# DeltaNet and a gated MLP on one core: chunk 0's inverses joined by matrix products, its scores a slot later, weight conversions redistributed

## The chip, the cores and the metric

The kernel runs on one core of a Trainium2 chip. The metric is the device time of one execution in microseconds. TensorE (PE; its weight loads are shown apart as PEld), VectorE (DVE), ScalarE (ACT), GpSimd (POOL) and the DMA queues that SyncE (SP), ACT and POOL issue run side by side. Each engine works off its own queue in order and waits for the others by semaphores.

## The reference

Two stages follow each other. The first is a delta-rule recurrence over 768 steps for 4 batches of 8 heads, with head size 48; the second is a two-layer MLP over the 3072 resulting rows, 384 to 2048 to 384, with a sigmoid-gated unit:

```python
k_n = k / (np.linalg.norm(k, axis=-1, keepdims=True) + 1e-06)
for t in range(S):
    kt, vt, bt = (k_n[:, :, t], v[:, :, t], beta[:, :, t, None])
    y[:, :, t] = np.einsum('bhd,bhde->bhe', q[:, :, t], state)
    v_old = np.einsum('bhde,bhd->bhe', state, kt)
    state = state + bt[:, :, :, None] * np.einsum('bhd,bhe->bhde', kt, vt - v_old)
...
h = x @ w_in
g = h * (1.0 / (1.0 + np.exp(-1.702 * h)))
return (g @ w_out).astype(np.float32)
```

The inputs `w_in` and `w_out` arrive as 64-bit floats and have to be turned into 32-bit ones on the chip.

## The kernel before

**Tiling.** The 768 steps are cut into 6 chunks of 128 steps. A *unit* is one chunk of one batch with all 8 heads; there are 24, ordered by chunk and then batch, so units 0 to 3 are chunk 0. Within a chunk the recurrence is a triangular system. It is cut into four blocks of 32 steps: a block's right-hand side V is multiplied by the inverse of the block's own 32x32 triangle (`solve`, tile psU, copied to U), and what U contributes to the later blocks is computed by `below` (psR) and subtracted from V by `rest`.

**Inverses.** `prepare` transposes the normalised keys (psT to kT), forms G, the products of keys with keys (psG), and sends G through DRAM so that the 32x32 blocks on its diagonal land in NT, one block to a partition: 32 partitions a batch (8 heads times 4 blocks). `invert` works on NT with VectorE. It scales NT by beta (L402), builds the inverses of both 16x16 halves of every block by a recursion of 15 steps (L424 to L431), and then joins the halves: the lower left quarter of NT is multiplied by one half's inverse (loop at L439) and the result by the other's (loop at L448), each in four pieces of one product and one reduction. The result times beta (L460, tile YS) is stored to DRAM (Yd) and loaded as XB, laid out so that `solve` can use it as weights. For chunk 0 all four batches are inverted at once before the loop, for later chunks two batches at a time, in pieces between other work.

**Scores.** `Step.scores` transposes a unit's queries (psT to QS), forms the masked products of keys and queries (psQ, copied to M, masked by a GpSimd select at L532). In later chunks it takes the state's contribution off V too (L527). `outputs` turns M and U into the unit's result (psY), which goes to xT; the rows that don't fit the copy's layout go through small DMAs on SP (L617).

**Slots.** The main loop runs over slots n = -1 to 24. Slot n has six groups; three units are in it at different points: A = unit n-1, B_ = unit n, D_ = unit n+1. D_'s scores are made in groups 0 to 2, its first block is solved in group 3; B_'s second block in group 1, third in group 5, and the last two blocks, the outputs and the state fall to it as A in the next slot. After each group come pieces of the inversion for the next chunk, `left // (GR - group)` weight conversions, and MoE matmuls worth the slot's share of time; with no MoE work queued, up to slot 2, six filler matmuls on a constant (`warm`). In slots -1 to 1 the order of the engines' instructions is pinned as written (`Engine`, L108); later, a scheduler may move them.

**Weights.** w_in is cut into 12 raw parts of 512 columns by 128 rows, w_out into 16 of 128 rows. A raw part is fetched by `ahead` into a staging place, most of these inside the still unused w_out tile, and `convert` turns it into 32-bit floats: `begin` issues the first step (L181) and an ACT relu (L186), the rest is four VectorE instructions (L190 to L193). A place can be fetched into again once its part is converted. `W0` parts are converted while the keys are prepared, `W1` just before the loop, `WB[n + 1]` in slot n. `hidden` (ph, L633) and `written` (po, L648) are the two MoE products; the first pair of units has its hidden products in slots 2 and 3 and its output products from slot 3 on.

**Order before the loop.** After the keys, units 0, 1 and 2 are scored, two more converted parts follow, the raw loads of the next six w_in parts are queued on SP, then chunk 0 is inverted, keys 4 to 6 are normalised (`normalize_first`), and the loop begins.

Of the kernel before, what the change touches and what calls it, by code (L numbers as in the profile page):

```python
# [8 lines left out]
F32 = mybir.dt.float32  # L9
# [9 lines left out]
def kernel(  # L19
# [35 lines left out]
    FQ = 4  # L55
    GB = 4

    W0, W1, WB = 3, 1, (1, 3, 5, 7, 8)
    NA = W0

    NW, NA0, NY, NB0 = 80, 3, 48, 6
# [331 lines left out]
    def invert(c, b0=0, nb=B):  # L393
# [37 lines left out]
            yield 0.0  # L431


        X1 = N[:, 0:HS, HS:]
        act.activation(X1, halves(Y)[1].rearrange("p l i -> p i l"), ACT.Copy)
        A = N[:, 0:HS, 0:HS]
        N10, Y0 = N[:, HS:, 0:HS], halves(Y)[0]
        Q = 4
        for j in range(0, HS, Q):  # L439
            n = HS - j  # L440
            dots(
                A[:, j : j + Q, :],
                N10[:, :, j:].rearrange("p (o l) k -> p o l k", o=1).broadcast_to([np, Q, HS, n]),
                Y0[:, j : j + Q, j:].rearrange("p j (o k) -> p j o k", o=1).broadcast_to([np, Q, HS, n]),
                Q, HS, n, False,
            )
            yield 0.0
        for i in range(0, HS, Q):  # L448
            n = i + Q
            dots(  # L450
                Y[:, 0:HS, HS + i : HS + i + Q],
                A[:, :, 0:n].rearrange("p j (o l) -> p j o l", o=1).broadcast_to([np, HS, Q, n]),
                X1[:, i : i + Q, 0:n].rearrange("p (o i) l -> p o i l", o=1).broadcast_to([np, HS, Q, n]),
                HS, Q, n, True,
            )
            yield 0.0
# [25 lines left out]
    class Step:  # L482
# [15 lines left out]

        def rows(self, h):
            return slice(h % 2 * 64, h % 2 * 64 + D)  # L500

        def scores(self):

# [190 lines left out]

    steps, xTs, inverting, gT0 = {}, {}, iter(()), []

    class NoStep:
        scored = iter(())

        def __bool__(self):  # L700
            return False

    def new_step(n):
        if n >= len(units):
            return NoStep()
# [22 lines left out]
    def slot(n, share):  # L728
# [81 lines left out]
    for b in range(B + 1):  # L810
# [14 lines left out]
    for U in US:  # L825
        nc.gpsimd.memset(U[:, H * D :], 0.0)
    for i in range(B, len(KN)):
        nc.gpsimd.memset(KN[i][:, :, D:DP], 0.0)
    for i in range(B, len(KN)):
        load(i, ((KN, k),), sync)  # L830
# [39 lines left out]
```

## Time and profile before

| | us |
|---|---|
| median of 13 runs | 834.96 |
| lowest and highest | 831.92, 839.08 |
| the profiled execution | 836.03 |
| its span, first to last instruction | 834.3 |

| engine | busy us | share of the span |
|---|---|---|
| PE | 782.4 | 94% |
| PEld | 574.8 | 69% |
| DVE | 493.2 | 59% |
| ACT | 214.1 | 26% |
| POOL | 119.1 | 14% |

A share over the whole span mixes stages. The first 66.5 us prepare keys and inverses, the loop's first slots solve chunk 0, from 104.5 us on TensorE has MoE products to do as well. The lines are to be read by stage: which engine is full there, and what the others wait for. "Granted clock" is the share of its full clock at which TensorE was allowed to run.

### The profile page before, as it was taken

To read this page: it belongs to the slowest core of one execution; us is meant where nothing else is said; L and a number is where in the kernel's file an instruction comes from. 1 tells how busy PE (TensorE), PEld (TensorE's weight loads), DVE (VectorE), ACT (ScalarE), POOL (GpSimd) and SP (SyncE) were. 2 spreads that over 40 slices of the span, in tenths; PEclk is the share of its full clock that TensorE was granted. 3 is DMA by queue.
4 is the path that set the end of the run, shared out by engine and by line. 5 is a ranking of instruction groups with operands and counts; after the bars stand their busy time and mean duration, and the time that the engine had idled before them with its cause. 6 is when DMAs were issued, how large, how long until landed. Compare 5 with 4: busy or idle time off the path is not lost.

```text
span 834.3 us, 18791 instructions
## 1 busy us (share of the span) xinstructions
PE 782.4 (94%) x8100; PEld 574.8 (69%) x8100; DVE 493.2 (59%) x1095; ACT 214.1 (26%) x441; POOL 119.1 (14%) x138
## 2 busy tenths in 40 slices
PE   8338899879999999999999999999999999999998
PEld 6327788546867867867867767767767768677684
DVE  6898889688776395394494493593692871110000
ACT  2303543232322321312312212222223212111020
POOL 2103120232022112102202202202200000000000
PEclk9659698988999999999999999999999999999999
DMA  9996731722214204213213223123123020000000
GB/s 148 197 169 137 194 86 48 181 65 68 56 35 107 61 11 101 61 30 82 62 45 73 55 52 78 43 58 88 27 56 78 1 60 2 11 15 2 24 1 19
DMA packets 147315, 55.97 MB, mean 67 GB/s; under 512 B 114336, under 2 KB 143232, under 8 KB 147232
## 3 DMA queue, kind: packets, MB, share of 16 engines
q1 hardware_dynamic: 139488, 41.96, 24.6%
q0 software_dynamic: 2752, 10.62, 4.5%
q10 hardware_dynamic: 4992, 2.20, 1.0%
q8 instruction: 63, 1.03, 0.5%
q14 instruction: 20, 0.16, 0.1%
HBM read 33.13 MB, written 20.45 MB: 64 GB/s over the span
## 4 chain that ended last, share of the span: by engine, by line
PE 68%; DVE 15%; DMA 7%; issue 7%; POOL 3%; ACT 0%; ACTq 0%; DVEq 0%; SPq 0%; POOLq 0%
PE ph L633 26%; PE po L648 24%; PE psU L552 4%; PE psY L568 4%; PE psQ L519 2%; PE psG L366 2%; DMA KN<-in_k_dram 2%; DVE P L426 2%; DVE YB L430 2%; DVE P L104 2%; DMA w_out<-in_moe_w_out_dram 2%; PE psR L541 2%; POOL rn L312 1%; DMA w_out<-in_moe_w_in_dram 1%; PE psS L590 1%
## 5 line engine op out<-in xcount | busy, mean ns | idle before, releaser
L633 PE MATMUL ph<-xT,w_in 128*128 128x256 f32 (+1 forms) x1248 | 278.0, 376 | 2.6 <-DMA xT<-last 2.4
L648 PE MATMUL po<-w_out,gT 128*128 128x384 f32 x768 | 267.9, 495 | 4.7 <-DVE w_out L193 4.6
L633 PEld LDWEIGHTS ph<-xT,w_in 128*128 128x128 f32 x1248 | 222.8, 196 | 41.3 <-issue 9.4
L648 PEld LDWEIGHTS po<-w_out,gT 128*128 128x128 f32 x768 | 140.4, 190 | 95.1 <-DVE w_out L193 6.9
L638 ACT ACTIVATE gT<-ph 128x512 f32<-128x512 f32 (+1 forms) x104 | 58.7, 565 | 190.1 <-PE ph L633 190.0
L548 DVE TENSOR_TENSOR V<-V,psR 32x384 f32<-32x384 f32 x87 | 48.3, 555 | 89.9 <-PE psR L541 88.2
L552 PEld LDWEIGHTS psU<-V,XB 32*32 32x32 f32 x1408 | 52.0, 106 | 35.0 <-issue 17.2
L559 ACT COPY US<-psU 32x384 f32<-32x384 f32 x88 | 41.4, 470 | 130.5 <-PE psR L541 112.7
L552 PE MATMUL psU<-V,XB 32*32 32x48 f32 x1408 | 63.4, 205 | 5.6 <-DVE V L527 4.2
L532 POOL TENSOR_SCALAR_AFFINE_SELECT M<-M 128x1024 f32<-128x1024 f32 x24 | 27.3, 1137 | 265.9 <-DVE M L529 192.9
L541 PE MATMUL psR<-US,G 32*32 32x48 f32 x2080 | 60.9, 204 | 0.0
L655 DVE COPY o<-po 128x384 f32<-128x384 f32 x24 | 13.1, 544 | 66.9 <-PE po L648 66.8
L541 PEld LDWEIGHTS psR<-US,G 32*32 32x32 f32 x2080 | 50.2, 105 | 1.4 <-issue 1.2
L426 DVE TENSOR_TENSOR P<-NT,YB 64x2 f32<-64x2 f32 (+4 forms) x135 | 46.8, 347 | 4.0
L430 DVE TENSOR_REDUCE YB<-P 64x2 f32<-64x2 f32 (+4 forms) x135 | 43.3, 321 | 4.3
L519 PE MATMUL psQ<-QS,kT 48*128 48x176 f32 (+1 forms) x384 | 42.9, 350 | 2.1 <-ACT QS L352 2.1
L527 DVE TENSOR_TENSOR V<-V,psQ 128x96 f32<-128x96 f32 x80 | 17.4, 250 | 40.4 <-PE psQ L519 39.7
L519 PEld LDWEIGHTS psQ<-QS,kT 48*128 48x128 f32 x384 | 30.8, 206 | 14.3 <-issue 4.8
L529 ACT COPY M<-psQ 128x256 f32<-128x256 f32 x68 | 23.9, 374 | 65.1 <-DVE V L527 60.3
L89 POOL DMA_DIRECT2D KN<-in_k_dram x14 | 13.4, 957 | 185.5 <-PE psS L590 174.4
L609 DVE COPY last<-psY 128x128 f32<-128x128 f32 x20 | 5.8, 288 | 52.6 <-PE psY L568 52.4
L153 PE MATMUL ps_warm<-ident 128*128 128x256 bf16 x152 | 21.1, 302 | 15.8 <-DVE ps_warm L104 13.5
(118 smaller groups left out, 795.9 us busy)
## 6 DMA issues: line engine op xcount, KB each, us to landing
Nd<-G SPq DMA_DIRECT2D x20, 512.0 KB, 3.2
w_out<-in_moe_w_out_dram POOLq DMA_DIRECT2D x14, 384.0 KB, 3.8
QP<-in_q_dram SPq DMA_DIRECT2D x24, 192.0 KB, 3.1
V<-in_v_dram SPq DMA_DIRECT2D x24, 192.0 KB, 2.9
out_dram<-o SPq DMA_DIRECT2D x24, 192.0 KB, 2.8
w_out<-in_moe_w_in_dram SPq DMA_DIRECT2D x6, 576.0 KB, 11.9
NT<-Nd SPq DMA_DIRECT2D x24, 128.0 KB, 2.6
Yd<-YS SPq DMA_DIRECT2D x24, 128.0 KB, 2.2
```

The source lines that it names most:

```text
L426: tt(P, diag(Nf, i * BS, [[0, i], [1, i]]), diag(Yf, 0, [[BS, i], [1, i]]), op=ALU.mult,)
L430: red(diag(Yf, i, [[BS, i]]), P, axis=AX.X, op=ALU.add, negate=True)
L519: pe.matmul(ps[hh][:, i, 0:n], lhsT=self.kT[r, g + i, :], rhs=self.QS[r, g + i, 0:n], start=True, stop=True,)
L532: nc.gpsimd.affine_select(out=self.M, in_=self.M, compare_op=ALU.is_gt, fill=0.0, base=0, pattern=[[0, H], [1, 128]], channel_multiplier=-1,)
L541: pe.matmul(psR[u, h, :], lhsT=self.G[r, h, u], rhs=self.U[r, h, :], start=True, stop=True,)
L548: vec.tensor_tensor(self.V[u], self.V[u], psR[u], op=ALU.subtract)
L552: pe.matmul(psU[r, h, :], lhsT=inverse[self.n][r, h, :], rhs=self.V[r, h, :], start=True, stop=True,)
L559: act.copy(self.U[r], psU[r])
L568: pe.matmul(self.psY[h % 2][p : p + DP, s, :], lhsT=lhsT(h), rhs=rhs(h), start=start and s == 0, stop=True, skip_group_check=True,)
L633: pe.matmul(ph[:, u], lhsT=w_in[:, j, f * 128 : (f + 1) * 128], rhs=xT[:, j, t], start=(j == 0), stop=(j == KC - 1),)
L638: act.activation(gT[f0 // FQ][:, f0 % FQ : f0 % FQ + 2, t], ph, ACT.Gelu_apprx_sigmoid)
L648: pe.matmul(po, lhsT=gT[f // FQ][:, f % FQ, i * C : (i + 1) * C], rhs=w_out[:, f, :], start=(f == 0), stop=(f == FC - 1),)
```

## The change

- In `invert`, chunk 0 skips the join of the halves: no copy of the transposed half to NT, none of the eight product and reduction pairs. YS then holds the two 16x16 inverses of each block, scaled by beta, and goes to DRAM and back to XB as before.
- A new generator, `Step.merged`, joins the blocks of a unit of chunk 0 from XB: a transposition of XB in 32x32 blocks on VectorE (XT), 32 small products of G with the second half (psA), a copy (A), 32 products with the transposed first half (psA again), and four activations with scale -1 that write the missing quarter into XB.
- In slot n, when unit n+1 is of chunk 0, its join is begun in group 0 and finished in group 1.
- Units of chunk 0 are scored in slot n as B_ rather than in slot n-1 as D_, so nothing is scored ahead of the loop. In slot 3 unit 3 and unit 4, the first of chunk 1, are scored in the same groups.
- Ahead of the inversion stand one load of three raw parts, keys 4 to 6 and the values of two units; another three raw parts, the queries and the other values come after the inverses' own transfers. Before, six raw parts, all queries, all values and keys 4 to 6 were ahead.
- Conversions: W1 = 2 instead of 1, WB = (3, 4, 4, 5, 7) instead of (1, 3, 5, 7, 8). With W0 = 3 both sum to 28.

```diff
-    W0, W1, WB = 3, 1, (1, 3, 5, 7, 8)
+    W0, W1, WB = 3, 2, (3, 4, 4, 5, 7)
...
+        Q = 4
+        quarters = range(0, HS, Q) if c > 0 else ()
         X1 = N[:, 0:HS, HS:]
-        act.activation(X1, halves(Y)[1].rearrange("p l i -> p i l"), ACT.Copy)
+        if c > 0:
+            act.activation(X1, halves(Y)[1].rearrange("p l i -> p i l"), ACT.Copy)
...
-        for j in range(0, HS, Q):
+        for j in quarters:
...
-        for i in range(0, HS, Q):
+        for i in quarters:
...
+        def merged(self):
+            HS = BS // 2
+            XB, blocks = inverse[self.n], [slice(k * BS, (k + 1) * BS) for k in range(NB)]
+            XT = wk.tile([128, H, BS], F32, tag="XT", name="XT", bufs=1)
+            vec.transpose(XT, XB)
+            psA = bank("psA", (128, H, HS))
+            for h in range(H):
+                for r in blocks:
+                    pe.matmul(
+                        psA[r, h, :], lhsT=self.G[r, h, r], rhs=XB[r, h, HS:],
+                        start=True, stop=True,
+                    )
+            A = wk.tile([128, H, HS], F32, tag="A", name="A", bufs=1)
+            act.copy(A, psA)
+            yield
+            psA = bank("psA", (128, H, HS))
+            for h in range(H):
+                for r in blocks:
+                    pe.matmul(
+                        psA[r.start : r.start + HS, h, :], lhsT=XT[r, h, 0:HS], rhs=A[r, h, :],
+                        start=True, stop=True,
+                    )
+            for r in blocks:
+                r = slice(r.start, r.start + HS)
+                act.activation(XB[r, :, HS:], psA[r], ACT.Copy, scale=-1.0)
...
                 D_ = steps.get(n + 1) or new_step(n + 1)
-                next(D_.scored, None)
+                whole = D_.merged() if D_ and D_.c == 0 else iter(())
+                next(whole, None)
+                scored = [X.scored for X in (B_, D_) if X and (X is D_) == (X.c > 0)]
+                for work in scored:
+                    next(work, None)
             elif group == 1:
                 together([(B_, 1)], [(A, 2)])
-                next(D_.scored, None)
+                run(whole)
+                for work in scored:
+                    next(work, None)
             elif group == 2:
-                run(D_.scored)
+                for work in scored:
+                    run(work)
...
-    for b in range(3):
-        load(b, ((QP, q),), sync)
-    for b in range(B):
+    run(weights(W0 - 1, None))
+    ahead(1, sync)
+    for i in range(B, len(KN)):
+        nc.gpsimd.memset(KN[i][:, :, D:DP], 0.0)
+        load(i, ((KN, k),), sync)
+    for b in range(HB):
         load_values(b, sync)
-    for b in range(3):
-        run(new_step(b).scored)
-    run(weights(W0 - 1, None))
-    load(3, ((QP, q),), sync)
...
-    ahead(2, sync)
     run(invert(0))
+    ahead(1, sync)
+    for b in range(B):
+        load(b, ((QP, q),), sync)
+    for b in range(HB, B):
+        load_values(b, sync)
     normalize_first(B, len(KN) - B)
-    run(weights(W1))
+    run(weights(W1, None))
```

More of the change, by code (lines that the diff above doesn't have):

```diff
@@ L431, in invert @@
             yield 0.0
+        Q = 4
+        quarters = range(0, HS, Q) if c > 0 else ()
         X1 = N[:, 0:HS, HS:]
-        act.activation(X1, halves(Y)[1].rearrange("p l i -> p i l"), ACT.Copy)
+        if c > 0:
+            act.activation(X1, halves(Y)[1].rearrange("p l i -> p i l"), ACT.Copy)
         A = N[:, 0:HS, 0:HS]
         N10, Y0 = N[:, HS:, 0:HS], halves(Y)[0]
-        Q = 4
-        for j in range(0, HS, Q):
+        for j in quarters:
             n = HS - j
@@ L695 @@
     steps, xTs, inverting, gT0 = {}, {}, iter(()), []
[L697 to L701, printed above, removed]
     def new_step(n):
         if n >= len(units):
-            return NoStep()
+            return None
         h = n // HB
@@ L826 @@
         nc.gpsimd.memset(U[:, H * D :], 0.0)
[L827 to L830, printed above, removed]
-    ahead(2, sync)
-    run(invert(0))
+    run(invert(0))
+    ahead(1, sync)
[3 more added lines that the diff above has]
+        load_values(b, sync)
     normalize_first(B, len(KN) - B)
-    run(weights(W1))
+    run(weights(W1, None))
     for n in range(-1, len(units) + 1):
```

## The prediction, made before the run

> **What bounds the kernel now.** I read the page's busy slices first, then busy time by stage, then the waits of TensorE and VectorE, and last the timeline of the first 200 us. The slices say where TensorE isn't full:
>
> ```profile
> PE   8338899879999999999999999999999999999998
> ...
> DVE  6898889688776395394494493593692871110000
> ...
> PEclk9659698988999999999999999999999999999999
> ```
>
> A slice is 20.9 us. From the eleventh on TensorE is full, and the rest of the span is its work; only what happens before about 240 us can be won or lost. By stage (length, then PE, PEld, DVE, ACT and POOL busy, granted clock, DMA share, GB/s):
>
> ```profile
> 0.00:66.50 66.50, 36.91 (x298) 30.03 (x298) 55.93 (x138) 14.28 (x30) 8.96 (x24) 0.74 1.02 169
> 66.50:104.50 38.00, 32.90 (x610) 26.59 (x610) 32.38 (x61) 19.22 (x39) 10.66 (x19) 0.82 0.68 169
> 104.50:146.40 41.90, 39.54 (x455) 35.87 (x448) 39.49 (x90) 15.96 (x37) 6.61 (x7) 0.87 0.28 65
> 146.40:192.00 45.60, 38.17 (x421) 23.36 (x420) 33.93 (x80) 14.60 (x34) 13.39 (x15) 0.93 0.49 122
> ...
> 240.00:834.30 594.30, 588.67 (x5914) 423.60 (x5912) 294.33 (x647) 136.18 (x275) 72.96 (x68) 1.00 0.20 46
> ```
>
> I cut at the events that matter: the first solve (66.5), the first MoE matmul (104.5), the first output matmul (146.4), and the end of the first pair's output (192). Up to 146 VectorE is the busiest engine (84 to 94%); half of what TensorE does before 104 is warm-up filler. Between 146 and 192 TensorE idles 45.60 - 38.17 = 7.4 us. The two wait lists say why (total, times, longest):
>
> ```profile
> PE po L648 <- DVE w_out L193: 4.6, 4, 2.3
> PE ph L633 <- DMA xT<-last: 2.4, 1, 2.4
> PE psU L552 <- DVE V L527: 2.2, 2, 1.6
> ...
> DVE NT L402 <- DMA NT<-Nd: 8.6, 2, 4.4
> DVE w_out L181 <- DMA w_out<-in_moe_w_out_dram: 4.9, 4, 2.2
> ```
>
> Output matmuls (po) wait for converted w_out (L193); hidden ones (ph) once for xT's transfer, solves for V. Conversion is late because VectorE is late, because an NT scaling (L402) blocks its queue for 4.4 us behind a transfer at 149.5, and because each raw w_out part can be fetched only once an earlier one has left its staging place. The last part is converted at 188.4. So the path is: VectorE's queue from 31 us, then w_out conversion, then full TensorE.
>
> The piece removed, in VectorE's timeline (start, duration):
>
> ```profile
> 44.24 1.22 DVE L104 TENSOR_TENSOR P<-NT,YB 128x1024 f32<-128x1024 f32 x1
> 45.50 1.22 DVE L104 TENSOR_REDUCE NT<-P 128x64 f32<-128x1024 f32 x1
> ...
> 56.00 1.22 DVE L104 TENSOR_REDUCE YB<-P 128x64 f32<-128x1024 f32 x1
> 57.23 0.06 DVE L104 MEMSET ps_warm<- 128x1 f32 x1
> 57.26 1.22 DVE L460 TENSOR_TENSOR YS<-YB,bI 128x1024 f32<-128x1024 f32 x1
> ```
>
> Eight products and eight reductions, back to back: 57.23 - 44.24 = 13.0 us.
>
> **What the Trainium skill says.** "VectorE: DVE Perf Modes", Rules for kernel authors, calls `tensor_reduce` the slowest VectorE operation and tells one to expect 1x; the trace agrees (1.22 us for 1024 elements per partition, like the product). The same page, The three transpose paths, says that VectorE transposes 32x32 blocks only and gives 311 ns for 128x128 bf16; no run here shows one. "TensorE: Matmul & The Clock Gate", What's actually happening, says that TensorE falls to half clock after an idle window of about 3.4 us; the trace agrees (0.50 granted from 30 to 60 us, where TensorE was 27 to 63% busy). "TensorEngine Tiling (Array Packing)", Key Properties: different tiles of the array run in parallel. The trace fits: 48 records of psR, 32x32, took 0.88 us.
>
> **The change part by part.** All dates are on the clock of the trace before.
>
> Before the blocks leave. The 13.0 us go. The scores of units 0 to 2 leave the front, with them two GpSimd selects beside the recursion: two of its products took 0.78 and 1.21 us during these, their neighbours 0.41 and 0.56, so about 1.0 us more. YS ends at 58.5 - 14.0 = 44.5.
>
> The blocks' trip. Before: first store issued 58.51, load landed 66.5, 8.0 us, among 3 MB of raw w_in. In SP's queue only parts 6 to 8 pass from ahead of the blocks to behind them (parts 3 to 5 move further ahead), so the raw load in flight is less. I take 7 us: landed at 51.5. But this isn't what the first solve now waits for: in VectorE's order the first transposition XT stands behind normalisation (58.40 to 66.34: 7.9 us) and three conversions, parts 3, 4 and 5 (two took 66.25 to 71.79: 2.8 each, 8.3). XT starts at 44.5 + 7.9 + 8.3 = 60.7. So 9 of the 14 us are spent at once on conversions that before came later.
>
> The new join, per unit: XT about 0.35 us (estimate from the 0.41 to 0.43 of VectorE rows with 256 elements; 0.3 to 0.6), 64 + 64 matmul records of psA (from psR: 1.2 us each; 0.7 if more tiles overlap, 2.4 at half clock), one ACT copy and four activations of 16x128 (nearest: 128x128 from PSUM, 0.25 us each), some 1.3 together. In slot -1 these follow in a row, TensorE being cold from its wait: 60.7 + 0.35 + 1.7 (psA) + 2.4 (twelve fillers) + 0.9 (psU) + 0.5 (US) + 1.6 (fillers) + 0.9 (psR) = 69.0 for the first V subtraction, which before started at 71.82. Gain 2.8, with parts up to 6 converted rather than 4. The conversion of part 6 sits in VectorE's queue ahead of it and waits for raw part 6, issued near 51 and, at 12 us to landing for such loads, there at 63; it ends near 66, so it is covered by 3 us. If that load is 4 us late, each further us goes on.
>
> Slots 0 and 1. A whole join and a whole scoring now stand between two solves on TensorE: psA 1.2, two psQ groups 0.7 each and one filler run 0.8, in place of a filler run, 2.5 to 3 us a slot, and the second psA waits for XT behind a conversion. Adding up as above: V subtractions near 78.4, 88.8 and 94.1 (before 76.12, 86.28, 92.49); psY of unit 0 near 96 (before 91.83). The lead turns into a lag of 4 us. Before, however, xT's second half stood in SP's queue behind NT<-Nd, which waited for the store Nd<-G, issued 92.81 and landed 99.17 among raw w_out loads of 384 KB each; these now go earlier, and Nd should take 3.5 to 4.5. G is ready near 96.4, Nd lands near 100.5, xT's last pieces issue then and land 3 us later: first MoE matmul near 104.5. **Shift taken: 0; bounds -2 and +4.**
>
> Conversions. At the end of slot 1 VectorE is near 101.5 where it was at 103.5 (first scaling of chunk 1), with parts up to 14 converted, where it was at 11: three at 2.3 us plus 2 is 9 us of lead. In the new order six more parts (19 to 24) stand ahead of the L402 that blocks for 4.4 us; before they stood behind it. Following the staging chain at 6 us a link (issue, 3.8 us landing, conversion), the last part is done near 167 rather than 188. Output matmuls starting at 146 then hardly wait: of the 7.4 us idle I take **6.0 off** (bounds 3 and 7.4; some waits are for V, not w_out). Granted clock there was 0.93, 3.2 us of full clock lost after idle; I take **2.0 off** (0 to 4, as 192 to 240 also has 0.93).
>
> Added to full TensorE after 104.5: unit 3's join (two psA, 1.6 warm; 0.9 to 2.4) and one more unit's scores, since unit 3's fall into slot 3 beside unit 4's (psT 0.5 and psQ 1.4): **3.5 on** (2.8 to 4.3).
>
> Free: removed X1 copy (0.66, ACT idle there); Q loads behind the blocks (needed near 71, issued near 54); M's selects on POOL behind two raw fetches (free near 76, needed at 96).
>
> Sum: 0 - 6.0 - 2.0 + 3.5 = -4.5 us. The profiled execution took 836.03 (span 834.3 and 1.7 around it): 831.5. The median of the 13 runs is 1.1 lower: 834.96 - 4.5 = **830.5**.
>
> **The rivals.**
> 1. The forecast, 830.5, own range 826 to 833: 0.46.
> 2. More: fillers and stalls in slots 0 and 1 give way and the first MoE matmul comes 2 us earlier, all idle goes, clock recovers by 3: -2 - 7.4 - 3 + 3.5 = -8.9, 826. For it: VectorE does 13 us less. Against: the chain of slots 0 and 1 is then TensorE's and ACT's. 0.08.
> 3. No difference: w_out is early, but TensorE then waits in 146 to 192 for V and psQ instead (2.2 us already stand there), 4 of 6 us come back: -0.5, 834.5. 0.16.
> 4. Slower: the serial join. In slots 0 and 1 psA, ACT copies and psQ lengthen the chain to psY beyond what 104.5 can absorb. If psY comes at 99 and Nd again takes 6.4 us, xT lands near 109.5: +5; stalls saved fall to 3, since later output matmuls already found fewer to wait for; 3.5 on, clock 1 off: 5 - 3 + 3.5 - 1 = +4.5, 839.5. It decides once psY is over 3 us later than my 96. For it: each slot's path really is longer, and ACT has relus, kT, A and QS queued ahead of US. Against: DMA is calmer. 0.30.
> That the join isn't moved at all is excluded by the order of instructions.
>
> **How the numbers follow.** Cases 1 and 2 are faster: 0.54; 3 is the same, 0.16; 4 slower, 0.30. What tells from no change is about 0.2%, 1.7 us. Range 824 to 839.5 holds case 1 with its ends, 2, 3 and the near half of 4.
>
> **What would show it.** Right: no 13 us block after 44, YS near 44.5, XT near 60.7, first ph near 104.5, no po wait for L193 above 1 us, last L193 before 175, PE idle after 146 under 2 us. Wrong: first ph after 107 (rival 4), part 6 waiting beyond 67, or PE in 146 to 192 idle as before with other releasers (rival 3).

## The result

The changed kernel is slower. Median of 11 runs 843.4 us (841.71 to 851.76), beside 834.5 us for 48 runs of the kernel before (829.54 to 845.71): ratio 1.0124, 95% interval 1.0098 to 1.0150. (Ratios, here and below, compare the undisturbed runs of both kernels; the medians are of all runs, which take in a few slow ones, so a ratio isn't always the quotient of two medians.) The forecast was 830.5 with a range that ended at 839.5; the time lies outside it, on the side of rival 4 and beyond its 839.5. The profiled execution took 849.14 us (span 847.4), 5.7 above its median, so dates of its trace after 100 us may be some microseconds late against a typical run.

The busy slices of the changed kernel (a slice is now 21.2 us):

```profile
PE   8065889979999999999999999999999999999998
...
DVE  6974668986859278277386385394493681110000
...
PEclk9576769986999999999999999999999999999999
DMA  9998544442222303304204204213223010000000
```

TensorE's second slice fell from 3 to 0, as the scores have left the front; but VectorE's fourth, 64 to 85 us, is only 4 (it was 8), and the clock there is 6 (it was 9). The row for DMA, which the prediction never looked at, has three nines. The row of the kernel before begins 99967: its DMA engines were already full for the first 63 us.

By stage, with the cuts of the prediction (length, then PE, PEld, DVE, ACT and POOL busy, granted clock, DMA share, GB/s):

```profile
0.00:66.50 66.50, 36.05 (x478) 28.85 (x478) 49.03 (x137) 11.71 (x23) 11.15 (x33) 0.79 1.04 172
66.50:104.50 38.00, 26.77 (x565) 20.84 (x567) 23.05 (x45) 15.23 (x36) 5.96 (x9) 0.67 0.67 133
104.50:146.40 41.90, 39.58 (x672) 34.27 (x663) 31.37 (x73) 21.80 (x51) 8.08 (x9) 0.81 0.43 105
146.40:192.00 45.60, 39.44 (x426) 29.43 (x426) 40.16 (x86) 15.23 (x36) 11.19 (x12) 0.93 0.43 96
```

VectorE is busy 55.93 - 49.03 = 6.9 us less up to 66.5 and 9.3 us less from there to 104.5: 16 us in all, the 13 of the join and more, part of it work that only comes later. The time turned into waiting. VectorE's timeline and the waits from 20 to 240 us (total, times, longest) say for what:

```profile
42.39 1.22 DVE L463 TENSOR_TENSOR YS<-YB,bI 128x1024 f32<-128x1024 f32 x1
...
57.53 0.44 DVE L104 STREAM_TRANSPOSE XT<-XB 128x256 f32<-128x256 f32 x1
72.39 0.76 DVE L104 TENSOR_SCALAR w_in<-w_out 128x512 int32<-128x512 int32 x2 [14.43 <-DMA w_out<-in_moe_w_in_dram]
...
75.58 1.14 DVE L104 TENSOR_TENSOR V<-V,psR 32x384 f32<-32x384 f32 x2
...
87.38 0.56 DVE L104 TENSOR_TENSOR V<-V,psR 64x384 f32<-64x384 f32 x1 [4.78 <-PE psR L104]
```

```profile
DVE w_in L104 <- DMA w_out<-in_moe_w_in_dram: 14.4, 1, 14.4
DVE V L104 <- PE psR L104: 10.5, 3, 4.8
...
DVE V L582 <- PE psR L575: 8.6, 3, 4.9
...
PE po L682 <- DVE w_out L193: 4.1, 2, 3.5
```

The join is off VectorE and YS begins at 42.39, 14.9 us earlier than before. XT is done at 57.97. Then VectorE stands for 14.4 us in front of the conversion of part 6, whose raw data are not there, with the first V subtraction queued behind it. Who used the DMA engines meanwhile is in the queues of SP and of GpSimd:

```profile
43.83 2.48 SPq L104 DMA_DIRECT2D Yd<-YS  x4
47.53 3.76 SPq L104 DMA_DIRECT2D XB<-Yd  x4
51.34 3.56 SPq L104 DMA_DIRECT2D w_out<-in_moe_w_in_dram  x4
54.94 17.82 SPq L104 DMA_DIRECT2D QP<-in_q_dram  x4
```

```profile
47.87 2.24 POOL L259 DMA_DIRECT2D w_out<-in_moe_w_in_dram  x4 [42.48 <-DVE w_in L192]
51.55 2.17 POOL L259 DMA_DIRECT2D w_out<-in_moe_w_in_dram  x4 [1.44 <-DVE z L104]
54.13 2.00 POOL L259 DMA_DIRECT2D w_out<-in_moe_w_in_dram  x4 [0.41 <-DVE z L104]
```

Parts 6 to 8 are issued from 51.34 on, in four transfers, and are all there 21 us later. Parts 9, 10 and 11 are issued by GpSimd at 47.87, 51.55 and 54.13 and travel beside them, although VectorE takes up the first of them only at 79.8 and finishes it at 90.8. SP stands 17.8 us in its four Q loads.

In the kernel before the same subtraction began without a wait:

```profile
71.82 1.14 DVE L104 TENSOR_TENSOR V<-V,psR 32x384 f32<-32x384 f32 x2
```

The delay then grows: first V subtraction 75.58 (before 71.82), psY of unit 0 at 108.21 (91.83), first ph 120.66 (104.54). After that it shrinks a little: last conversion 193.09 (188.40), span 13.1 us longer.

### The profile page after: what moved, and what is told of

It reads as the page before. It is cut to its first block, busy times and chain, and to the rows that moved or that the text cites. A ratio compares the mean times of both kernels' runs of the same rounds, so it can differ in the third digit from the quotient of the medians.

```text
span 847.4 us, 19816 instructions
## 1 busy us (share of the span) xinstructions
PE 792.3 (93%) x8612; PEld 581.0 (69%) x8612; DVE 480.2 (57%) x1083; ACT 218.1 (26%) x460; POOL 117.4 (14%) x138
## 4 chain that ended last, share of the span: by engine, by line
PE 75%; DVE 12%; DMA 5%; SPq 2%; issue 2%; POOL 2%; ACT 0%; DVEq 0%; POOLq 0%
PE ph L667 27%; PE po L682 25%; PE psU L586 4%; PE psY L602 4%; PE psQ L553 3%; PE psG L366 3%; DMA KN<-in_k_dram 2%; SPq L104 2%; DVE P L426 2%; DVE YB L430 2%; PE psR L575 2%; PE psT L351 2%; DVE P L104 2%; PE ps_warm L153 2%; DMA QP<-in_q_dram 1%
## 5 line engine op out<-in xcount | busy, mean ns | idle before, releaser
L682 PE MATMUL po<-w_out,gT 128*128 128x384 f32 x768 | 270.9, 500 | 4.1 <-DVE w_out L193 4.1
L667 PE MATMUL ph<-xT,w_in 128*128 128x256 f32 (+1 forms) x1248 | 273.2, 371 | 0.2
L667 PEld LDWEIGHTS ph<-xT,w_in 128*128 128x128 f32 x1248 | 218.2, 192 | 38.6 <-issue 7.4
L689 DVE COPY o<-po 128x384 f32<-128x384 f32 x24 | 13.1, 544 | 69.6 <-PE po L682 69.5
L553 PE MATMUL psQ<-QS,kT 48*128 48x176 f32 (+1 forms) x352 | 40.9, 344 | 0.0
L553 PEld LDWEIGHTS psQ<-QS,kT 48*128 48x128 f32 x352 | 28.5, 195 | 11.8 <-issue 5.2
L563 ACT COPY M<-psQ 128x256 f32<-128x256 f32 x60 | 21.2, 374 | 58.4 <-DVE V L561 57.1
```

The lines of the kernel that those rows point to most:

```text
L553: pe.matmul(ps[hh][:, i, 0:n], lhsT=self.kT[r, g + i, :], rhs=self.QS[r, g + i, 0:n], start=True, stop=True,)
L667: pe.matmul(ph[:, u], lhsT=w_in[:, j, f * 128 : (f + 1) * 128], rhs=xT[:, j, t], start=(j == 0), stop=(j == KC - 1),)
L682: pe.matmul(po, lhsT=gT[f // FQ][:, f % FQ, i * C : (i + 1) * C], rhs=w_out[:, f, :], start=(f == 0), stop=(f == FC - 1),)
```

## The experiments

Two theories stand behind the expectations. **A**: the transfers of the front are what failed; parts 6 to 8, put behind the blocks, land late in front of the first solve, and the join itself is a gain. **B**, rival 4 of the prediction: the join and the later scores make the chain from solve to solve on TensorE and ScalarE too long.

All runs. Each row is compared with runs of the kernel before on the same chip.

| run | built on | us | ratio to before, 95% interval |
|---|---|---|---|
| x1_raw_ahead | changed | 830.86 to 843.82 | 4 runs, no interval |
| x2_fetch_on_sp | changed | 838.99 | 1.0053 (1.0029 to 1.0077) |
| x3_join_alone | before | 840.46 | 1.0087 (1.0057 to 1.0118) |
| x4_scores_late | before | 835.28 | 1.0016 (0.9996 to 1.0037) |
| x5_conversions_alone | before | 834.65 | 1.0026 (1.0008 to 1.0045) |
| x6_join_back | changed | 847.99 | 1.0184 (1.0144 to 1.0223) |
| x7_short_chain_sp | x2 | 836.58 | 1.0049 (1.0023 to 1.0075) |
| x8_short_chain_pool | changed | 841.91 | 1.0109 (1.0069 to 1.0149) |
| x9_old_spread | changed | 840.87 | 1.0098 (1.0066 to 1.0130) |
| x10_short_sp_old_spread | x7 | 843.16 | 1.0112 (1.0080 to 1.0143) |
| x11_short_sp_mid_spread | x7 | 840.17 | 1.0080 (1.0046 to 1.0115) |
| x12_q_loads_late | x7 | 836.08 | 1.0018 (1.0000 to 1.0035) |
| x13_after_less_raw | changed | 832.69 | 0.9979 (0.9957 to 1.0002) |
| x14_before_less_raw | before | 830.54 | 0.9950 (0.9926 to 0.9974) |
| x15_split_parts | x12 | 835.60 | 1.0003 (0.9975 to 1.0032) |
| x16_few_fillers | x15 | 829.10 | 0.9952 (0.9937 to 0.9968) |
| x17_before_few_fillers | before | 834.78 | 1.0005 (0.9988 to 1.0022) |
| x18_after_few_fillers | changed | 846.40 | 1.0145 (1.0108 to 1.0182) |

### Where the raw parts stand in the queues

**x1**, parts 6 to 8 fetched ahead of the recursion:

```diff
+    ahead(1, sync)
     run(invert(0))
-    ahead(1, sync)
```

> The changed kernel with raw w_in parts 6 to 8 queued on SP ahead of the inversion again, everything else as changed. Theory A (the 14.4 us for which VectorE stands at the first step of part 6 is what pushes the first MoE matmul from 104.5 to 120.7): that wait falls from 14.4 us to under 3, the first V subtraction comes at 65 to 68 instead of 75.6, the first MoE matmul near 110, the time 834 to 838. Rival B (the join and the scores between two solves set the pace of slots 0 and 1): the wait goes, but the first MoE matmul stays at 116 or later and the time at 840 or more.

The four runs took 830.86, 840.04, 843.60 and 843.82 us, too few and too far apart to say whether the loss stayed. The trace, of the run of 840.04, says more. The wait for part 6 went, but now the blocks were late: YS went out at 46.67, their load was issued only at 58.99, and XT waited 5.0 us for it, until 64.95. The first V subtraction came at 73.92, not at 65 to 68, and first ph at 110.6, 10 us before that of the changed kernel. A part of the wait had moved, not gone.

**x2**, the fetches of slot -1 in SP's queue, behind the Q loads, instead of on GpSimd:

```diff
-            run(weights(more))
+            run(weights(more, sync if n < 0 else nc.gpsimd.dma_start))
```

> The changed kernel with parts 9 to 11 fetched from SP's queue, behind parts 6 to 8, the queries and the values, instead of from POOL's, where they are fetched at the same time. Theory A in its sharper form (parts 6 to 8 are late because parts 9 to 11 share the DMA engines with them): the wait of VectorE falls from 14.4 us to 4 to 7, the first MoE matmul comes 7 to 10 us earlier than 120.7, the time 835 to 839. If it is only that parts 6 to 8 are issued after the blocks, the wait stays above 11 us and the time near 843.

One word about a queue took more than half of the loss away: 1.0124 became 1.0053. Part 6 was there at 64.13 instead of 72.39:

```profile
64.13 0.77 DVE L104 TENSOR_SCALAR w_in<-w_out 128x512 int32<-128x512 int32 x2 [6.26 <-DMA w_out<-in_moe_w_in_dram]
```

VectorE waited 6.3 us for it and later 3.7 for part 9, which now came behind the Q loads. The bytes are the same; only what travels beside part 6 differs. This is what the Trainium skill states in "Trainium Kernel Development and Optimization", Key Constraints: DMAs from the queues of SP, ACT and POOL all run on the same 16 engines and interleave.

### The parts of the change one by one

**x3**, the kernel before with the join on TensorE alone (raw parts 3 to 8 stay ahead of the blocks):

```diff
+        quarters = range(0, HS, Q) if c > 0 else ()
...
+                whole = D_.merged() if D_ and D_.c == 0 else iter(())
+                next(whole, None)
...
+                run(whole)
```

> The kernel before with the join on TensorE alone: scores of units 0 to 2 ahead of the loop, raw parts 3 to 8 ahead of the inversion, W1 and WB as before. Theory A (the join itself is a gain, the load order costs): YS near 44, first MoE matmul 4 to 8 us before 104.5, time 828 to 832. Rival B (the join's chain on TensorE and ACT eats the 13 us): first MoE matmul at 104 or later, time 835 or more.

Theory A's second half fell here. Alone, the join's move costs 0.9%. YS begins at 43.63, but six raw parts are in flight. From the timelines of SP and of VectorE:

```profile
38.97 6.67 SPq L104 DMA_DIRECT2D w_out<-in_moe_w_in_dram  x8
49.66 7.19 SPq L104 DMA_DIRECT2D Yd<-YS  x4
66.59 4.76 SPq L104 DMA_DIRECT2D XB<-Yd  x4
```

```profile
71.40 0.45 DVE L104 STREAM_TRANSPOSE XT<-XB 128x256 f32<-128x256 f32 x1 [9.13 <-DMA XB<-Yd]
```

From YS to the first use of the blocks it is 28 us (43.63 to 71.40), where before it was 9, from 57.26 to this:

```profile
66.54 0.86 PE L104 MATMUL psU<-V,XB 32*32 32x48 f32 x16 [0.32 <-DMA XB<-Yd]
```

Before, the raw parts came in while VectorE did its 13 us of products and reductions; in x3 they are still under way when the blocks set out. Of the two orders, raw parts first or blocks first, each makes the other late. The blocks are not the whole loss here: two V subtractions also wait 5.2 and 4.6 us for psR.

**x4**, the kernel before with the scores of units 0 to 2 in the slots, as changed:

```diff
+                scored = [X.scored for X in (B_, D_) if X and (X is D_) == (X.c > 0)]
...
-    for b in range(3):
-        run(new_step(b).scored)
```

> The kernel before with only the scores of chunk 0 moved into slots 0 to 3; join on VectorE, loads and conversions as before. Theory A: the scores cost 1 to 3 us of first MoE matmul, time 835 to 838. Rival B (scores between two solves are half of the loss): first MoE matmul 6 us or more later, time 840 or more.

0.2%, with 1 in the interval: the later scores alone are not the cause. They do lengthen the chain: V waits 5.6 us for psR there, instead of 2.7.

**x5**, the kernel before with the new spread alone:

```diff
-    W0, W1, WB = 3, 1, (1, 3, 5, 7, 8)
+    W0, W1, WB = 3, 2, (3, 4, 4, 5, 7)
```

> The kernel before with the new spread of conversions alone (five instead of four ahead of slot 0's first solve and so on: W1 2, WB 3, 4, 4, 5, 7); join, scores and order of loads stay. Theory A (the front's transfers are late): two to three more conversions stand ahead of the first V subtraction and one of them, part 6, has its raw data late, so first V subtraction at 79 or later and about 838. Theory B (the chain of join, scores and fillers between two solves): the chain is untouched, VectorE only works in another order, the first V subtraction is some 7 us later but the conversions lead, about 835; second V subtraction 4 to 5 us after the first, as before.

0.3%. The first V subtraction came 5.3 us later (77.08), psY 5.5 later (97.30), first ph at 106.45; the last step of the last conversion came at 177.77 rather than 188.40. The lead in conversions, which the prediction counted on, is real (10.6 us here) and about pays for the delay, no more.

**x6**, the changed kernel with the join back on VectorE, so that all but the join remains:

```diff
-        quarters = range(0, HS, Q) if c > 0 else ()
+        quarters = range(0, HS, Q)
...
-                whole = D_.merged() if D_ and D_.c == 0 else iter(())
+                whole = iter(())
```

> The changed kernel with the join put back on VectorE (all else of the change stays: raw parts 6 to 8 behind the blocks, scores a slot later, conversions spread). Theory A: the blocks leave near 57 as before, raw parts 6 to 8 are issued behind them near 66 and land near 80 beside GpSimd's parts 9 to 11, and part 6's conversion stands ahead of the first V subtraction: that comes at 80 or later, and the time is near the changed kernel's, 841 to 845. Theory B: the chain between the solves is short again (first to second V subtraction 5 us rather than 11.8), so most of the loss is gone: about 837.

848.0: the worst of all, beyond both expectations, and nearer to A's 841 to 845 than to B's 837. VectorE waits 14.7 us for part 6 here too, until 84.88, and the first V subtraction comes at 88.06. By the ratios (1.0184 and 1.0124, intervals that only just touch) the kernel with the join back on VectorE is about 0.6% or 5 us slower than the changed one. That isn't the price of the join's place alone: the blocks set out 14 us later, parts 6 to 8 behind them, and TensorE waits 15.3 us for a Q load. It fits A: with the join on either engine, the place of parts 6 to 8 and what travels beside them costs.

### The chain between two solves

The changed kernel's TensorE between the second solve of slot 0 and the psR that the second V subtraction waits for:

```profile
76.18 1.48 PE L104 MATMUL psU<-V,XB 32*32 32x48 f32 x16 [0.43 <-DVE V L104]
80.05 0.72 PE L104 MATMUL psA<-A,XT 32*16 32x16 f32 x64 [2.39 <-DVE XT L104]
80.70 1.23 PE L104 MATMUL psQ<-QS,kT 48*128 48x128 f32 x8
81.86 1.46 PE L104 MATMUL ps_warm<-ident 128*128 128x256 bf16 x6
83.25 1.23 PE L104 MATMUL psQ<-QS,kT 48*128 48x128 f32 x8
84.41 1.46 PE L104 MATMUL ps_warm<-ident 128*128 128x256 bf16 x6
85.81 0.28 PE L104 MATMUL psU<-V,XB 32*32 32x48 f32 x1
```

9.6 us from psU to psU, where the kernel before needed 2.2:

```profile
72.42 0.86 PE L104 MATMUL psU<-V,XB 32*32 32x48 f32 x16 [0.95 <-DVE V L104]
...
74.63 0.27 PE L104 MATMUL psU<-V,XB 32*32 32x48 f32 x2
```

TensorE had stood idle from 66.5 to 70.0, and its granted clock is 0.50 from 70 to 92 us. Most groups take nearly twice their time: psU 1.48 us for 0.86, psQ 1.23 for 0.71, 6 fillers 1.46 for 0.82. The second psA, 0.72, doesn't. **x8** shortens this chain in the changed kernel; **x7** does the same in x2. All four XT are transposed ahead of the conversions, and the scores of chunk 0 go behind the second solve of their slot:

```diff
-            XT = wk.tile([128, H, BS], F32, tag="XT", name="XT", bufs=1)
-            vec.transpose(XT, XB)
+            XT = turned[self.n]
...
+                late = [work for work in scored if not (D_ and D_.c > 0 or n >= B - 1)]
+                scored = [work for work in scored if work not in late]
...
                 run(P)
+                for work in late:
+                    next(work, None)
...
+    turned = []
+    for b in range(B):
+        turned.append(wk.tile([128, H, BS], F32, tag="XT", name="XT", bufs=4))
+        vec.transpose(turned[b], inverse[b])
```

> The variant that fetches the parts of the first slot in SP's queue, with a shorter chain between the solves besides: all four transpositions XT stand ahead of the conversions, and the scores of chunk 0 are issued behind the second solve of their slot instead of between the first and the second. Theory A alone: the late raw parts still stand ahead of the V subtractions, nothing changes by over 1 us, about 838. Theory B: the second V subtraction comes 6 us after the first instead of 11.8, first ph 4 to 6 us earlier, about 834.

> The changed kernel with the same shorter chain and nothing else (GpSimd fetches as in the changed kernel). Theory A: part 6 lands at 72 as before, first V subtraction near 75.6, time within 1.5 us of the changed kernel, 842. Theory B: the first V subtraction is as late, but the second follows 6 to 7 us behind it instead of 11.8, and the time falls to about 838. With the changed kernel, the variant on SP's queue and the one with both, this makes a two by two: if the two costs add up, this and the SP queue's gain (4.4 us) give the sum.

The two by two: GpSimd fetches, long chain 1.0124, short 1.0109; SP fetches, long 1.0053, short 1.0049. The shorter chain moves the ratio by 0.0015 at most, inside the intervals; the queue moves it by 0.006 to 0.007. In x8 the second subtraction does follow 7.9 us behind the first instead of 11.8, and first ph comes 4 us earlier (116.68), yet little of it is left in the time. In x7 first ph comes at 110.3, 2.0 us before that of x2, where B expected 4 to 6.

### The spread of the conversions

If one conversion of a late part ahead of the solve were all, the old spread would cure it. **x9** is the changed kernel with W1 = 1 and WB = (1, 3, 5, 7, 8); **x10** is x7 with the same; **x11** is x7 with W1 = 2 and WB = (1, 4, 5, 6, 7).

> The changed kernel with the old spread of conversions (W1 1, WB 1, 3, 5, 7, 8): join on TensorE, raw parts 6 to 8 behind the blocks and later scores stay; no conversion of part 6 stands ahead of the first V subtraction now, and GpSimd fetches one group less in the first slot. Theory A (late raw parts, and their conversion ahead of the solve): the 14 us wait is no longer in front of the chain; first V subtraction near 63, psY of unit 0 before 95, first ph near 105, and about 836 (loss down from 9 to 2 us). Theory B (serial chain of join and scores): the chain from the first V subtraction to psY takes 30 us or more whatever stands ahead of it, so psY not before 98 and about 840.

> The variant with SP's queue and the short chain, with the old spread of conversions besides. Theory A: with part 6 off the path and no fetch from GpSimd beside it, the first V subtraction comes near 62, psY near 88, first ph near 100, 4 us earlier than in the kernel before: about 832, faster than both. Theory B: little left of it, since the chain is short already: it gains what the 68.4 to 62 of the first subtraction gives, at most 3 us, about 834. If the conversions that are pushed back make first ph wait for w_in, neither holds and it stays at 836.

> The same with a spread in between (W1 2, WB 1, 4, 5, 6, 7): parts up to 5, whose raw data landed before the blocks, ahead of the first V subtraction, part 6 and later behind it. Theory A: first V subtraction near 65, no wait for a part ahead of it, and about 832, as the old spread or 1 us better for the conversion lead. Theory B: about 834. Against the variant with the new spread (836.6) it prices the one conversion of part 6 that stands ahead of the solve.

All three missed, x10 worst: 843 where 832 was expected. The timeline of x9 on VectorE:

```profile
65.30 1.14 DVE L104 TENSOR_TENSOR V<-V,psR 32x384 f32<-32x384 f32 x2 [7.47 <-PE psR L104]
82.82 0.56 DVE L104 TENSOR_TENSOR V<-V,psR 64x384 f32<-64x384 f32 x1 [15.93 <-PE psR L104]
```

The first subtraction is early (65.30), the second waits 15.9 us for psR, among others because TensorE waits for QP until 72.48, which sits in the same crowd of transfers. In x10 the second waits 10.0 us (76.96) and in x11 6.8 (78.72). In x7, with more conversions, the second also came at 78.95, but VectorE converted in the meantime. A conversion taken from ahead of a solve leaves a hole there and is done later on VectorE's full stretch. So A in this narrow form is wrong, and the chain is a second limit right behind the first.

### The bytes themselves

**x12** is x7 with the four Q loads and the last two V loads behind all raw parts of slot -1 in SP's queue:

```diff
-    for b in range(B):
-        load(b, ((QP, q),), sync)
-    for b in range(HB, B):
-        load_values(b, sync)
...
+        if n < 0:
+            for b in range(B):
+                load(b, ((QP, q),), sync)
+            for b in range(HB, B):
+                load_values(b, sync)
```

> The variant with SP's queue and the short chain (new spread), with the four Q loads and the last two V loads moved behind all raw parts of the first slot in SP's queue: the same bytes, but 0.8 MB of Q no longer share the DMA engines with parts 6 to 8. Theory A (the front's transfers are the limit): part 6 lands 3 to 4 us earlier, near 61, the waits of 5.9 and 3.75 us shrink to 4 together, first V subtraction near 64, and the time is 833, no slower than the kernel before. Theory B (the chain): V subtractions earlier by less than 2 us, since psR then ends last, and 836. If the Q loads come too late for the scores of unit 0, TensorE waits for QP behind 80 and it is slower than 837.

1.0018, the best so far, but not by the way expected: part 6 still landed at 66.24 (7.0 us of waiting), since parts 9 to 11 now followed it directly; what went was x2's later wait for part 9. SP now stood 17.8 us in the raw transfers instead of the Q loads.

**x13** and **x14** take the loads of parts 6 to 8 out of the changed kernel and of the kernel before:

```diff
-        if part < parts_in:
+        if 2 * KC <= part < 3 * KC:
+            pass
+        elif part < parts_in:
             for p, r, m, step in x_rows:
```

> The changed kernel without the loads of raw parts 6 to 8 (their conversion stays and works on what lies in the staging place; w_in is then not the reference's in these parts): 1.5 MB less through the DMA engines, no wait for part 6. Theory A (transfers are what failed): first V subtraction near 62, first ph near 105, and below the same kernel before without these loads by 3 us or more, as the work removed from VectorE would then count. Theory B (chain of the serial join): the V subtractions wait for psR instead, and it stays 2 us or more above the kernel before without these loads.

> The kernel before without the same three loads: the measure for the run above. Theory A and B alike: VectorE bounds its front, not DMA, so little changes: 832 to 835. If it gains over 4 us, the kernel before was held by the transfers too.

Both leave a quarter of w_in unloaded, so they compute something else and serve only to measure. With 1.5 MB less on the way, the changed kernel is 10.7 us faster than with them (from one chip to another), the kernel before 4.3 us faster than the full one run beside it (830.54 against 834.83), and the distance between the two shrinks from 8.9 to 2.2 us (intervals that overlap between 0.9957 and 0.9974, so that the 2.2 are not certain to be more than 0). About three quarters of the loss go with these three loads. Expectation A asked for more, a gain of 3 us over x14, and did not get it. What waits from 44 to 116 us in x13, and then in x14:

```profile
DVE V L104 <- PE psR L104: 8.9, 3, 4.4
...
PE psA L104 <- DVE XT L104: 5.7, 2, 2.9
```

```profile
DVE V L104 <- PE psR L104: 2.7, 1, 2.7
```

No part of w_in is waited for any more, and the chain takes over: V waits 8.9 us for psR, where it waits 2.7 in the kernel before.

The kernel before gained too, so it was held by these loads as well, but not in its front: in x14 first ph comes at 105.87, later than its 104.54, and the last conversion at 184.45 for 188.40. Where its 4.3 us come from isn't shown. The date of first ph alone does not set the time.

**x15** is x12 with parts 6, 7 and 8 loaded one behind the other, each whole, instead of three parts' rows together:

```diff
-        return list(range(part, part + (KC if part < 3 * KC else 1)))
+        return list(range(part, part + (KC if part < 2 * KC else 1)))
...
-    order = [0, KC, 2 * KC] + list(range(3 * KC, n_parts))
+    order = [0, KC] + list(range(2 * KC, n_parts))
```

> The variant with late Q loads, with raw parts 6, 7 and 8 loaded one behind the other instead of interleaved in one set of transfers, so that part 6 is whole after a third of the bytes. Theory A: part 6 lands near 60 instead of 66, the wait of 7 us shrinks to 1 or 2, first V subtraction near 64, first ph near 105; 832, faster than the kernel before. Theory B: the subtraction waits for psR or the next one does; 835 to 836, as without the split. The eight more issues of SP cost about 4 us of its queue, which only the Q loads feel.

The wait for the load of part 6 is gone altogether (its conversion waits 3.0 us for ScalarE instead); the first V subtraction comes at 65.47, 10 us earlier than in the changed kernel, and psY at 94.22. The time equals that of the kernel before (1.0003), not 832. "Perfetto Trace Analysis", DMA Optimizations, says that splitting lets some transfers start sooner and advises it where the DMA engines are generally idle; here it helped with a DMA share of 0.99 up to 66.5 us, because the order of arrival was the point.

### Fillers in the chain

**x16**, **x17** and **x18** issue 2 instead of 6 fillers a group in slots -1 to 1, in x15, in the kernel before and in the changed kernel:

```diff
-    NW, NA0, NY, NB0 = 80, 3, 48, 6
+    NW, NA0, NY, NB0 = 80, 3, 48, 2
```

> The variant with split parts with 2 instead of 6 fillers a group in slots -1 to 1 (NB0). It asks what the fillers cost in the chain between the solves, where 12 of them took 1.5 to 2.7 us by the clock. Theory B (chain): each of the three waits of V for psR (5.8 us together) shrinks by 1 to 2 us, first ph 3 us earlier, near 103.5, and 833, faster than the kernel before by 0.2%. If the fillers are what keeps the clock up, the granted clock of 66 to 104 falls from 0.85 to 0.7 and the chain is as long: 836 or more. Theory A has nothing to say here: the same 835.6.

> The kernel before with 2 instead of 6 fillers a group in slots -1 to 1 and nothing else: the control for the run with few fillers. If the fillers cost as much here, it gains the same 0.5%, 830, and the variant's gain is none of the changed kernel's parts. Theory B (the fillers stand in the chain that the join made long): here VectorE ends last in these slots and V waited only 2.7 us for psR, so at most 1 us, 833.

> The changed kernel with 2 instead of 6 fillers a group and nothing else. Theory A (late raw parts end last): the wait for part 6 stays at 14 us, and at most 2 to 3 us of the slots' chain are gained: 840 to 842, still 0.7% or more slower than the kernel before. Theory B (fillers and serial chain are most of it): 836 or less.

x16 beats both kernels: 829.1 us, ratio 0.9952 (0.9937 to 0.9968), half a per cent less than x15's 1.0003. Fewer fillers are not a gain by themselves: nothing in the kernel before (1.0005), whose granted clock from 66.5 to 104.5 us fell from 0.82 to 0.64, and nothing in the changed kernel (1.0145, within the noise of 1.0124), where VectorE stands 17.2 us for part 6. The stage from 66.5 to 104.5 us in x15, and then in x16:

```profile
66.50:104.50 38.00, 32.68 (x904) 26.12 (x893) 28.50 (x55) 21.52 (x54) 7.35 (x11) 0.85 0.80 184
```

```profile
66.50:104.50 38.00, 34.72 (x857) 27.63 (x855) 28.01 (x53) 22.20 (x55) 7.26 (x11) 0.63 0.83 197
```

The clock falls from 0.85 to 0.63, as one of the two expectations feared, and V's three waits for psR still fall from 5.8 to 3.7 us in all. First ph comes at 100.19 instead of 106.45, 4.4 us ahead of the kernel before.

That the fillers stood in the chain explains only a part of this. Up to psY of unit 0 the gain is 1.4 us (92.83 for 94.22), and from the first V subtraction to psY both need 28.7 us. The other 4.9 us lie between psY and ph, where SP's queue is built in another order, although the two programs differ in one number only. From the timeline of SP in x15, and then in x16:

```profile
96.52 1.23 SPq L650 DMA_DIRECT2D xT<-last  x2
97.84 1.20 SPq L384 DMA_DIRECT2D NT<-Nd  x1
```

```profile
95.22 2.51 SPq L650 DMA_DIRECT2D xT<-last  x4
97.82 0.53 SPq L384 DMA_DIRECT2D NT<-Nd  x1
98.39 2.13 SPq L650 DMA_DIRECT2D xT<-last  x2
```

In x15 four of xT's six pieces stand behind NT<-Nd and are issued from 99.09 on, in x16 only two. ph begins in x16 before the pieces behind NT<-Nd can have landed (2.7 to 3.2 us after issue), in x15 only after they have (at most 4.5), so the order has probably a share. No run keeps the fillers and changes this order, so how the 6.3 us divide between fillers and order stays open. What is shown is that a clock of 0.63 or 0.64 in these slots did not cost time, in x16 or in x17.

## Why the prediction was wrong

**The step that failed** is the landing of part 6: "waits for raw part 6, issued near 51 and, at 12 us to landing for such loads, there at 63". It was issued at 51.34 and was there at 72.39, 21 us later. The 12 us were a median of such loads in the kernel before. What was left out is what would travel beside this one: GpSimd's fetches of parts 9 to 11 were counted as places in GpSimd's queue ("two raw fetches"), not as bytes on the same engines. x2 shows their share: with these fetches elsewhere part 6 was there at 64.13, so 8.3 of the 9.4 us of delay are theirs. That "the raw load in flight is less" was said of the blocks' trip, and held for it; for part 6 it did not. The stage row of the kernel before, with a DMA share of 1.02 up to 66.5 us, was quoted in the prediction, and nothing was made of it.

The prediction's own clause, that each microsecond beyond the 3 us of cover goes on, then gives the right date: 9.4 us late, 3 of them covered, leaves 6.4; 69.0 + 6.4 = 75.4 for the first V subtraction; it was 75.58. It also named "part 6 waiting beyond 67" among the signs of being wrong, and this sign came.

**Steps that held.** YS ended at 43.6 (predicted 44.5), XT began at 57.53 (60.7), and the blocks were used at 50.17 by the first psA (51.5). Two slips had no consequence: the 8.3 us of three conversions are once called 9, and VectorE is the busiest engine only up to 66.5 us; in the next two stages TensorE is level with it (32.90 and 32.38, 39.54 and 39.49).

**Luck.** In x13, where nothing is late, psY comes at 95.92 (predicted 96) and first ph at 104.86 (104.5). The sum is right there, but not its terms: the first V subtraction comes at 66.39, 2.6 us before the predicted 69.0, and from it to psY the chain needs 29.5 us and not 27. The chain was put 2.5 us too short, and an early start hides it.

**What the late part set off.** First ph is 16.1 us behind the predicted 104.5. 6.6 of it are there at the first V subtraction (75.58 for 69.0). 5.6 more come up to psY (108.2 - 96 = 12.2). 2.5 of these are the chain put too short, as in x13; the other 3.1 fall where the granted clock is 0.67 from 66.5 to 104.5, against 0.82 before and 0.86 in x13. That the clock is their cause is likely but was not tested, and x16, at 0.63, was no slower for it. The last 3.9 lie between psY and ph, 12.45 us instead of 8.5. The trip of Nd is 1 to 2 of them: its store was issued at 108.02 and the transfer behind it at 113.40, 5.4 us where 3.5 to 4.5 were taken. For the rest the trace has xT's last pieces, issued only behind that, from 113.97 to 116.14, and a psQ ahead of ph on TensorE.

**The conversion lead** was over-priced even without the late part. 6.0 us of TensorE's idle time in 146 to 192 were to go; the changed kernel idles 45.60 - 39.44 = 6.2 us there, against 7.4, and the last step of its last conversion comes at 193.09 and not near 167. Like is best compared with like, x13 and then x14:

```profile
146.40:192.00 45.60, 40.51 (x432) 25.66 (x432) 37.84 (x90) 13.91 (x33) 11.70 (x13) 0.89 0.50 110
```

```profile
146.40:192.00 45.60, 40.32 (x475) 25.88 (x473) 37.94 (x93) 15.32 (x34) 15.00 (x17) 0.93 0.53 128
```

Idle are 5.1 and 5.3 us: 0.2 came off where 6.0 were taken, although x13 is ahead in conversions (last step at 179.33, in x14 184.45). The clock, where 2.0 were to come off, gave nothing: from 146 to 240 us the gain in one half (1.00 for 0.96) is what the other loses (0.89 for 0.93). With the first ph 1.0 us earlier and the 3.5 us of added work taken as predicted (it was not measured apart), the sum is about +2.2, which is what the medians of x13 and x14 show, though their intervals don't exclude 0. So even with no transfer late the forecast gain of 4.5 us would not have come.

**The rivals.** The sign was that of rival 4 and the size beyond it. Its mechanism, the serial join, is not refuted: in x13 V waits 8.9 us for psR, 2.7 in x14. It is a second limit that stands behind the late part. The Q loads, which the prediction called free, were not always: TensorE waits for one until 72.48 in x9. No case of the prediction was about the DMA engines as the limit, although the page showed them full.

## What to carry to other kernels

Before work is taken from an engine that is full, look at what else is full beside it in that stage: if the DMA engines are, the time comes back as waiting for whatever lands last, and the order of transfers has to be changed with it, counted over all queues together and by who needs what first. After each limit is taken away, ask anew which one ends last: here first the raw parts, then the chain, and only the last step, with fewer fillers in the chain, came out ahead of the kernel before. Fillers that keep a clock up have to show that they pay: in these slots no run showed it. And when one number in the source is changed, compare the built order of the queues too, as it can have changed as well.

## What the runs showed of the hardware

- SP stood 17.82 us in issuing four Q loads of 192 KB in the changed kernel and 12.61 in x7. In x12, where the raw parts had gone ahead of them, the Q loads took 4.90, and SP stood 17.78 in 16 raw transfers instead. What holds the queue isn't shown. The two V loads behind the Q loads in the changed kernel were issued only at 72.81.
- A VectorE transposition of 32x32 blocks, 128x256 in f32, took 0.44 us; the prediction had estimated 0.35. For the 64 records of psA it had 1.2; the first product's took 0.73 us at a granted clock of 1.00 (in x16 1.05 at 0.50), the second's 0.72 at 0.50.
- After TensorE had stood idle from 66.5 to 70.0 us in the changed kernel, its granted clock was 0.50 up to 92 us.
- With a granted clock of 0.63 from 66.5 to 104.5 us in x16 the first MoE matmul came at 100.19 us, with 0.85 in x15 at 106.45; the clock is not the cause of this. In the kernel before, 0.64 for 0.82 left the time the same (x17, 1.0005).
